# Loading w_down of a decode kernel in three transfers instead of one, two of them issued by GpSimd

## The chip, the cores and the metric

The kernel runs on one core of a Trainium2 chip. The metric is device time in microseconds of one execution, given as the median of several executions. A profile of one execution stands beside the times; its span runs from the first to the last instruction that the profiler records, and is a little shorter than the time.

## The reference

A decode step for two tokens (B = 2, D = 512): the input is normalised, goes in parallel through an attention over a window of a cache and through a gated feed-forward layer, and both are added to the input. All data are float32.

```python
xn = layernorm(x)                                  # x: [2, 1, 512]
# attention: 32 query heads, 8 kv heads, head size 128, the last W = 4096 of 32768 positions
q = (xn @ wq) as [2, 32, 1, 128]                   # wq: [512, 4096]
p = softmax(q @ k_window^T * 128 ** -0.5)
a = (p @ v_window) as [2, 1, 4096] @ wo            # wo: [4096, 512]
# feed-forward, F = 1792
gate = xn @ W_gate                                 # [512, 1792]
gate = gate * (gate > 0)
up = xn @ W_up                                     # [512, 1792]
f = (gate * up) @ W_down                           # W_down: [1792, 512]
out = x + a + f
```

## The kernel before

All large inputs (wq in two halves, w_gate, w_up, 8 tiles of k, 8 tiles of v, w_down and two halves of wo) are loaded by SyncE into one ring of four slots (pool `ring`, RING = 4), each slot of 32 KB in each of the 128 partitions. A load waits on SyncE until the last reader of the tile that had the slot before is done; since SyncE issues in program order, the order of the loads is that of the code: wq0, wq1, w_gate, w_up, then k and v tiles in turn, the last two v tiles, w_down (`wd`), wo0 and wo1. wo1 is cut into five pieces of 8, 4, 2, 1 and 1 blocks (L434). The small input x is loaded by ScalarE (L105). GpSimd makes constants at the start (L113 to L134) and has nothing else to do.

The order of the instructions is that of the code (`manual_schedule`); semaphores are put in by the framework.

The stages, with the names that the profile shows:

- Normalisation and transposition of x (`xt_ps`, L177 to L182), then the query projection (`q_ps`, L190).
- The feed-forward's first part: `g_ps` and `u_ps` (L217) hold gate and up, with a quarter of the 1792 columns in each group of 32 partitions (row 32c + b of the tile is token b, quarter c, FQ = 448 columns). `gr` (L224) is the gate after its comparison, `hh` (L226) the product with up. 56 small matmuls against the identity (L231), for k in 0..13 and quarter c, turn hh into `ht_ps`, where partition p and block k hold hidden unit 14 p + k. The copy at L234 puts it into `hT`, a constant tile of [128, 14, 2, 16] that was set to zero by GpSimd (L120), where only index 0 of the last dimension is filled.
- For each of four groups g = (half of the kv heads, token): 8 x 8 transposes of each k tile (`pk`, L255) with copies by ScalarE and VectorE in turn (`kT`, L244), scores (`s`, L268), softmax (L277 to L321), products with the v tile (`o`, L332), and gathering (`oa`, L348). The scores of one group run beside the softmax and values of the one before.
- The end: `project` (L419) multiplies 17 columns of a block of hT or oT with the matching block of w_down or wo and sums all into one PSUM tile `y_ps`, whose first term is x. First come the values of the last group, then the 14 blocks of w_down (L429), then `spread_heads` (`op`, L362) for the last heads, then 16 blocks of wo0 and 16 of wo1. `yo` (L438) is the copy out of PSUM, and SyncE stores it (L439).

w_down is loaded by `load_down` (L82), one transfer: partition p takes the 14 rows 14 p to 14 p + 13, which lie one behind the other in memory (28 KB).

Of the kernel before, what the change touches and what calls it, by code (L numbers as in the profile page):

```python
# [9 lines left out]
F32 = mybir.dt.float32  # L10
AF = mybir.ActivationFunctionType
ALU = mybir.AluOpType
# [8 lines left out]
def kernel(  # L21
# [12 lines left out]
    nc = tc.nc  # L34
    P = 128
    B, _, D = x.shape
# [3 lines left out]
    F = w_gate.shape[1]  # L40
# [14 lines left out]
    FB = F // P  # L55
    FQ = F // Q
    assert (B, REP, DH, S1, J) == (2, 4, P, 2, 64)

    const = ctx.enter_context(tc.tile_pool(name="const", bufs=1))
    ring = ctx.enter_context(tc.tile_pool(name="ring", bufs=RING))  # L60
    ktp = ctx.enter_context(tc.tile_pool(name="ktp", bufs=2))
    work = ctx.enter_context(tc.tile_pool(name="work", bufs=2))
    ps_kt = ctx.enter_context(tc.tile_pool(name="ps_kt", bufs=3, space=PSUM))
    ps_s = ctx.enter_context(tc.tile_pool(name="ps_s", bufs=1, space=PSUM))
    ps_1 = ctx.enter_context(tc.tile_pool(name="ps_1", bufs=1, space=PSUM))
# [3 lines left out]
    def load(name, src, shape):  # L69
        t = ring.tile(shape, F32, name=name, tag="ring")  # L70
        nc.sync.dma_start(t, src)
        return t
# [6 lines left out]
    def load_ff(w, name):  # L79
        return load(name, w.rearrange("(p k) f -> p k f", p=P), [P, KC, F])  # L80

    def load_down():  # L82
        return load("wd", w_down.rearrange("(p k) e -> p k e", p=P), [P, FB, D])

    def load_kv(cache, name, g, a):
        r, b = divmod(g, B)
# [21 lines left out]
    ident = const.tile([P, P], F32, name="ident")  # L108
# [7 lines left out]
    eps_t = const.tile([32, 1], F32, name="eps_t")  # L116
    nc.vector.memset(eps_t, EPS)

    hT = const.tile([P, FB, B, 16], F32, name="hT")
    nc.gpsimd.memset(hT, 0.0)  # L120
    oT = const.tile([P, R, NJ, B, 16], F32, name="oT")
    nc.gpsimd.memset(oT, 0.0)
# [52 lines left out]
    for kc in range(KC):  # L175
        m, k = divmod(kc, 2)
# [9 lines left out]
    for kc in range(KC):  # L186
        for r in range(R):
            for c in range(C):
                n = r * C + c
                nc.tensor.matmul(  # L190
                    q_ps[r][32 * c:32 * c + 32, :], xnT[:, 0, kc, :], wqt[kc // 2][:, kc % 2, n * 512:(n + 1) * 512],
                    start=(kc == 0), stop=(kc == KC - 1),
# [3 lines left out]
    for r in range(R):  # L196
        qs = work.tile([P, 512], F32, name=f"qs{r}", tag="qs")
# [15 lines left out]
    u_ps = ps_kt.tile([P, FQ], F32, name="u_ps", tag="kt")  # L213
    for dst, wt in ((g_ps, gw), (u_ps, uw)):
        for kc in range(KC):
            for c in range(Q):
                nc.tensor.matmul(  # L217
                    dst[32 * c:32 * c + 32, :], xnT[:, 1, kc, :], wt[:, kc, c * FQ:(c + 1) * FQ],
                    start=(kc == 0), stop=(kc == KC - 1),
# [2 lines left out]
    nc.scalar.copy(gs, g_ps)  # L222
    gr = work.tile([P, FQ], F32, name="gr", tag="gr", bufs=1)
    nc.vector.scalar_tensor_tensor(gr, gs, 0.0, gs, op0=ALU.is_gt, op1=ALU.mult)  # L224
    hh = work.tile([P, FQ], F32, name="hh", tag="qs")
    nc.vector.tensor_tensor(hh, gr, u_ps, op=ALU.mult)  # L226
    ht_ps = ps_1.tile([P, FB, B], F32, name="ht_ps", tag="misc")
    hv = hh.rearrange("p (w k) -> p k w", k=FB)
    for k in range(FB):
        for c in range(Q):  # L230
            nc.tensor.matmul(  # L231
                ht_ps[32 * c:32 * c + 32, k], hv[:, k], ident[:, 32 * c:32 * c + B], start=True, stop=True
            )
    nc.vector.tensor_copy(hT[:, :, :, 0], ht_ps)  # L234

# [115 lines left out]
    def finish(g):  # L353
        r, b = divmod(g, B)
        if b == 0:
            osb[r] = const.tile([HR, B, P], F32, name=f"osb{r}")
        nc.vector.tensor_scalar(osb[r][:, b], oa[g], rls[g], 2.0, op0=ALU.mult, op1=ALU.mult)

    def spread_heads(r):
        op = ps_1.tile([P, NJ, B], F32, name=f"op{r}", tag="misc")  # L360
        for e in range(NE):
            nc.tensor.matmul(  # L362
                op, spread[:, e].rearrange("h k e -> h (k e)"),
                osb[r][:, :, e * NJ:(e + 1) * NJ].rearrange("h b j -> h j b"),
                start=(e == 0), stop=(e == NE - 1),
            )
        nc.vector.tensor_copy(oT[:, r, :, :, 0], op)
# [34 lines left out]
    scores(*pend.pop())  # L402
    vin = [load_kv(v_cache, "v", g, a) for a in range(NP)]
    dw = load_down()
    for _ in softmax(g):
        pass
# [10 lines left out]
    def project(lhsT, w, stop):  # L417
        for e in range(Q):
            nc.tensor.matmul(  # L419
                y_ps[32 * e:32 * e + 17, :], lhsT.rearrange("p b s -> p (b s)")[:, 0:17],  # L420
                w[:, e * P:(e + 1) * P], start=False, stop=stop,
            )
# [2 lines left out]
        values(g, a, vin[a])  # L425
        gather(g, a)
    finish(g)
    for k in range(FB):
        project(hT[:, k], dw[:, k], False)  # L429
    spread_heads(R - 1)  # L430
    for r, cuts in ((0, (0, NJ)), (1, (0, 8, 12, 14, 15, NJ))):
        wt = ring.tile([P, NJ, D], F32, name=f"wo{r}", tag="ring")
# [35 lines left out]
```

## Time and profile before

| what | us |
|---|---|
| median of 3 runs | 232.58 (232.47 to 232.73) |
| profiled execution | 232.63 |
| its span | 230.8 |
| TensorE busy | 180.2 |
| VectorE busy | 66.3 |
| ScalarE busy | 48.3 |
| GpSimd busy | 5.4 |

The page of the profile gives busy times of each engine, a table of the DMA queues (packets, megabytes and the time that packets took, as a share of the 16 load engines over the span), the chain of work that ended last, and groups of instructions by line. q1 is the queue that SyncE fills, q10 ScalarE's, and the queues of kind "instruction" bring the program itself. TensorE appears as PE (matmuls) and PEld (weight loads), VectorE as DVE, ScalarE as ACT, GpSimd as POOL, SyncE as SP; the letter q behind a name is the engine's instruction queue. A float32 matmul of the code appears as two instructions.

### The profile page before, as it was taken

How to read it: one execution, taken by the hardware profiler on the slowest of the kernel's cores; microseconds unless marked ns; L12 is line 12 of the kernel's file. 1: busy time of each engine (PE TensorE's matmuls, PEld its weight loads, DVE VectorE, ACT ScalarE, POOL GpSimd, SP SyncE). 2: the span in 40 equal slices, each digit the busy share in tenths (PEclk: the TensorE clock that was granted, in tenths of full speed). 3: DMA queues.
4: the chain of work that ended last, by engine and by line, in shares of the span. 5: the costliest groups of instructions: out<-in, count | busy, mean ns of one | idle time of the engine just before them, and what ended most of it. 6: DMA issues, size and time to landing. Idle time of an engine off the chain costs nothing.

```text
span 230.8 us, 4036 instructions
## 1 busy us (share of the span) xinstructions
PE 180.2 (78%) x1828; PEld 109.7 (48%) x1828; DVE 66.3 (29%) x131; ACT 48.3 (21%) x81; POOL 5.4 (2%) x21
## 2 busy tenths in 40 slices
PE   0066961749999889998899699889979964888393
PEld 0031230249666573664483566458456522247281
DVE  0320021014444561441472233158034133010000
ACT  2000100004444551440351243044033102100000
POOL 8000000000000000000000000000000000000000
PEclk9999797697999999999999799999999998899678
DMA  7999999999999999999999999999999999999980
GB/s 273 426 403 443 437 432 411 454 435 415 420 452 426 420 423 450 420 429 420 435 432 430 426 432 426 429 437 426 429 426 440 420 437 435 417 435 420 406 341 35
DMA packets 3964, 95.21 MB, mean 413 GB/s; under 512 B 452, under 2 KB 460, under 8 KB 876
## 3 DMA queue, kind: packets, MB, share of 16 engines
q1 hardware_dynamic: 3900, 94.90, 96.4%
q8 instruction: 14, 0.23, 0.4%
q10 hardware_dynamic: 48, 0.07, 0.1%
q14 instruction: 2, 0.02, 0.0%
HBM read 94.96 MB, written 0.00 MB: 412 GB/s over the span
## 4 chain that ended last, share of the span: by engine, by line
DMA 52%; PE 40%; DVE 4%; issue 1%; SPq 1%; ACT 1%
DMA k<-in_A_k_cache_dram 37%; PE pk L255 21%; DMA wo<-in_A_wo_dram 11%; PE s L268 8%; PE o L332 5%; DMA x<-in_A_x_dram 4%; PE q_ps L190 3%; PE pp L312 1%; PE oa L348 1%; SPq L434 1%; DVE kT L244 1%; DVE pt L313 1%; ACT p L301 1%; DVE on L244 0%; DVE m L277 0%
## 5 line engine op out<-in xcount | busy, mean ns | idle before, releaser
L255 PE MATMUL pk<-ident,k 128*128 128x128 f32 x512 | 68.0, 287 | 6.4 <-DMA k<-in_A_k_cache_dram 6.3
L255 PEld LDWEIGHTS pk<-ident,k 128*128 128x128 f32 x512 | 58.2, 146 | 21.2 <-issue 17.1
L244 DVE COPY kT<-pk 128x512 f32<-128x512 f32 x64 | 44.2, 691 | 52.6 <-PE pk L255 46.7
L244 ACT COPY kT<-pk 128x512 f32<-128x512 f32 x64 | 37.5, 586 | 81.5 <-PE pk L255 81.5
L332 PE MATMUL o<-v,pt 128*32 128x512 f32 x256 | 31.0, 615 | 0.0
L268 PE MATMUL s<-kT,qz 128*32 128x512 f32 x256 | 30.9, 598 | 0.0
L332 PEld LDWEIGHTS o<-v,pt 128*32 128x32 f32 x256 | 11.0, 113 | 14.6 <-issue 9.9
L190 PE MATMUL q_ps<-wq,xnT 128*32 128x512 f32 x64 | 11.9, 914 | 2.8 <-DMA wq<-in_A_wq_dram 2.3
L419 PE MATMUL y_ps<-wo,oT 128*17 128x128 f32 x256 | 10.1, 323 | 5.0 <-DMA wo<-in_A_wo_dram 4.8
L268 PEld LDWEIGHTS s<-kT,qz 128*32 128x32 f32 x256 | 7.0, 109 | 11.9 <-issue 11.5
L348 PE MATMUL oa<-on,pick 128*16 128x128 f32 x64 | 8.3, 273 | 4.1 <-DVE on L244 3.3
L419 PEld LDWEIGHTS y_ps<-wo,oT 128*17 128x17 f32 x256 | 7.9, 116 | 7.0 <-DMA wo<-in_A_wo_dram 6.0
L244 DVE COPY on<-o 128x512 f32<-128x512 f32 x4 | 2.8, 692 | 29.0 <-PE o L332 29.0
L348 PEld LDWEIGHTS oa<-on,pick 128*16 128x16 f32 x64 | 5.8, 97 | 11.1 <-DVE on L244 7.0
L177 PE MATMUL xt_ps<-ident,xn 32*128 32x32 f32 x4 | 1.0, 299 | 12.9 <-DVE xn L172 12.9
L217 PE MATMUL u_ps<-wu,xnT 128*32 128x448 f32 x32 | 4.6, 735 | 6.3 <-DMA wu<-in_B_W_up_dram 6.3
L190 PEld LDWEIGHTS q_ps<-wq,xnT 128*32 128x32 f32 x64 | 2.7, 154 | 11.3 <-issue 7.1
L244 ACT COPY on<-o 128x512 f32<-128x512 f32 x4 | 2.3, 586 | 25.5 <-PE o L332 25.5
L301 ACT ACTIVATE p<-s,nm 128x1024 f32<-128x1024 f32 x4 | 4.5, 1115 | 12.5 <-DVE nm L296 12.5
L177 PEld LDWEIGHTS xt_ps<-ident,xn 32*128 32x128 f32 x4 | 0.8, 206 | 12.8 <-issue 12.8
L312 PE MATMUL pp<-ident,p 128*128 128x128 f32 x32 | 4.9, 279 | 2.4 <-ACT p L301 1.5
L313 DVE TENSOR_TENSOR pt<-pp,own 128x512 f32<-128x512 f32 x8 | 5.4, 690 | 3.4 <-PE pp L312 3.4
(71 smaller groups left out, 61.5 us busy)
## 6 DMA issues: line engine op xcount, KB each, us to landing
k<-in_A_k_cache_dram SPq DMA_DIRECT2D x8, 4096.0 KB, 29.2
v<-in_A_v_cache_dram SPq DMA_DIRECT2D x8, 4096.0 KB, 31.2
wq<-in_A_wq_dram SPq DMA_DIRECT2D x2, 4096.0 KB, 17.5
wo<-in_A_wo_dram SPq DMA_DIRECT2D x1, 4096.0 KB, 31.5
wg<-in_B_W_gate_dram SPq DMA_DIRECT2D x1, 3584.0 KB, 30.2
wu<-in_B_W_up_dram SPq DMA_DIRECT2D x1, 3584.0 KB
wd<-in_B_W_down_dram SPq DMA_DIRECT2D x1, 3584.0 KB, 27.9
wo<-in_A_wo_dram SPq DMA_DIRECT2D x1, 2048.0 KB, 21.6
```

Of the source, the lines that this page charges most:

```text
L190: nc.tensor.matmul(q_ps[r][32 * c:32 * c + 32, :], xnT[:, 0, kc, :], wqt[kc // 2][:, kc % 2, n * 512:(n + 1) * 512], start=(kc == 0), stop ...
L217: nc.tensor.matmul(dst[32 * c:32 * c + 32, :], xnT[:, 1, kc, :], wt[:, kc, c * FQ:(c + 1) * FQ], start=(kc == 0), stop=(kc == KC - 1),)
L244: (nc.vector.tensor_copy if turn[0] % 2 else nc.scalar.copy)(dst, src)
L255: nc.tensor.transpose(pk[:, u * P:(u + 1) * P], kt_in[:, j * P:(j + 1) * P], ident)
L268: nc.tensor.matmul(ss[g][32 * q:32 * q + 32, :], qz[:, g, 32 * n:32 * n + 32], kt[:, h, q * 512:(q + 1) * 512], start=(a == 0 and s1 == 0 ...
L301: nc.scalar.activation(p, both, AF.Exp, bias=nm, scale=SCALE, accum_out=l)
L312: nc.tensor.transpose(pp[:, u], pv[:, lo:lo + P], ident)
L313: nc.vector.tensor_tensor(pts[g][:, jh].rearrange("p n u k -> p u n k"), pp.rearrange("p u (n k) -> p u n k", k=HK), own.rearrange("p h i ...
L332: nc.tensor.matmul(o[32 * q:32 * q + 32, :], pts[g][:, jh, n].rearrange("p u k -> p (u k)"), v[:, lo:lo + 512], start=(s1 == 0 and jh == 0 ...
L348: nc.tensor.matmul(oa[g], pick[:, u, 8 - 8 * a:24 - 8 * a], ons[a][:, u], start=(a == 0 and u == 0), stop=(a == NP - 1 and u == 3),)
L419: nc.tensor.matmul(y_ps[32 * e:32 * e + 17, :], lhsT.rearrange("p b s -> p (b s)")[:, 0:17], w[:, e * P:(e + 1) * P], start=False, stop=stop,)
L434: nc.sync.dma_start(wt[:, j0:j1], wo_rows(r, j0, j1))
```

## The change

The 1792 rows of w_down are divided otherwise. They are cut into 16 runs of 112 rows (FR). Of each run the first 104 rows go to eight partitions, 13 rows (FM) in each, by one transfer that SyncE issues as before. The last 8 rows of each run, 128 rows in all, become blocks 13 and 14 of the lower 64 partitions: two transfers of 64 rows (8 runs of 8 rows), one row of 2 KB in a partition, both issued by GpSimd. The tile has 15 blocks for 14, and so has hT.

The hidden units must lie in the same order, so hh is written already ordered: one product for the 13 blocks, another for the last 8 columns of each run; the transposing matmuls of block 13 put quarters 0 and 1 into block 13 and quarters 2 and 3 into block 14, both in the lower 64 partitions; and the copy into hT becomes two. At the end `project` runs over 15 blocks, the last two with 64 rows.

```diff
+    FR = F // 16
+    FM = FB - 1
     def load_down():
-        return load("wd", w_down.rearrange("(p k) e -> p k e", p=P), [P, FB, D])
+        t = ring.tile([P, FB + 1, D], F32, name="wd", tag="ring")
+        runs = w_down.rearrange("(i x) e -> i x e", i=16)
+        main = bass.AP(
+            tensor=w_down.tensor, offset=w_down.offset, ap=[[FR * D, 16], [FM * D, 8], [1, FM * D]]
+        )
+        nc.sync.dma_start(t[:, 0:FM].rearrange("p k e -> p (k e)"), main)
+        for s in range(2):
+            nc.gpsimd.dma_start(t[0:64, FM + s], runs[8 * s:8 * s + 8, 8 * FM:, :])
+        return t
...
-    hT = const.tile([P, FB, B, 16], F32, name="hT")
+    hT = const.tile([P, FB + 1, B, 16], F32, name="hT")
...
-    hh = work.tile([P, FQ], F32, name="hh", tag="qs")
-    nc.vector.tensor_tensor(hh, gr, u_ps, op=ALU.mult)
-    ht_ps = ps_1.tile([P, FB, B], F32, name="ht_ps", tag="misc")
-    hv = hh.rearrange("p (w k) -> p k w", k=FB)
+    hh = work.tile([P, FB, 32], F32, name="hh", tag="qs")
+    gv = gr.rearrange("p (i x) -> p i x", i=4)
+    uv = u_ps.rearrange("p (i x) -> p i x", i=4)
+    nc.vector.tensor_tensor(
+        hh[:, 0:FM].rearrange("p k (i y) -> p i y k", i=4), gv[:, :, 0:8 * FM].rearrange("p i (y k) -> p i y k", y=8),
+        uv[:, :, 0:8 * FM].rearrange("p i (y k) -> p i y k", y=8), op=ALU.mult,
+    )
+    nc.vector.tensor_tensor(
+        hh[:, FM].rearrange("p (i y) -> p i y", i=4), gv[:, :, 8 * FM:], uv[:, :, 8 * FM:], op=ALU.mult
+    )
+    ht_ps = ps_1.tile([P, FB + 1, B], F32, name="ht_ps", tag="misc")
     for k in range(FB):
         for c in range(Q):
+            s = c // 2 if k == FM else 0
             nc.tensor.matmul(
-                ht_ps[32 * c:32 * c + 32, k], hv[:, k], ident[:, 32 * c:32 * c + B], start=True, stop=True
-            )
-    nc.vector.tensor_copy(hT[:, :, :, 0], ht_ps)
+                ht_ps[32 * (c - 2 * s):32 * (c - 2 * s) + 32, k + s], hh[:, k], ident[:, 32 * c:32 * c + B],
+                start=True, stop=True,
+            )
+    nc.vector.tensor_copy(hT[:, 0:FM, :, 0], ht_ps[:, 0:FM])
+    nc.vector.tensor_copy(hT[0:64, FM:, :, 0], ht_ps[0:64, FM:])
...
-    for k in range(FB):
-        project(hT[:, k], dw[:, k], False)
+    for k in range(FB + 1):
+        n = P if k < FM else 64
+        project(hT[0:n, k], dw[0:n, k], False)
```

More of the change, by code (lines that the diff above doesn't have):

```diff
@@ L80, in load_ff @@
         return load(name, w.rearrange("(p k) f -> p k f", p=P), [P, KC, F])
+    FR = F // 16
+    FM = FB - 1
+    assert FR == 8 * FM + 8
     def load_down():
-        return load("wd", w_down.rearrange("(p k) e -> p k e", p=P), [P, FB, D])
+        t = ring.tile([P, FB + 1, D], F32, name="wd", tag="ring")
[7 more added lines that the diff above has]
+        return t
     def load_kv(cache, name, g, a):
```

## The prediction

> **What bounds the kernel now.** I read the queue table of the page first, then the chain of waits at its end, then the stages by window.
>
> ```profile
> span 230.8 us, 4036 instructions
> ...
> PE 180.2 (78%) x1828; PEld 109.7 (48%) x1828; DVE 66.3 (29%) x131; ACT 48.3 (21%) x81; POOL 5.4 (2%) x21
> ...
> ## 3 DMA queue, kind: packets, MB, share of 16 engines
> q1 hardware_dynamic: 3900, 94.90, 96.4%
> q8 instruction: 14, 0.23, 0.4%
> q10 hardware_dynamic: 48, 0.07, 0.1%
> ```
>
> The load engines are busy for 96.4% of the span with SyncE's queue q1 alone. That is 0.964 x 230.8 = 222.5 us in each of 16 engines for 94.90 MB, so 26.7 GB/s for one engine, and 16 KB takes 0.61 us. No compute engine comes near that share. The end of the chain says the same.
>
> ```profile
> 202.21 24.94 DMA wo<-in_A_wo_dram
> 227.15 0.04 issue
> 227.19 0.46 PE y_ps L419 x8
> 227.65 0.02 issue
> 227.68 0.29 DVE yo L438
> ```
>
> The last piece of wo is issued at 202.21 and lands 24.94 us later, because all earlier loads stand ahead of it in the queues. After it come 0.8 us of TensorE and VectorE, and the store of the output. So the time is set by when the last load engine has finished its list, and the windows show how the engines finish (the last two columns are the busy share of the 16 engines and GB/s).
>
> ```profile
> core 0: us, PE busy (x) PEld busy (x) DVE busy (x) ACT busy (x) POOL busy (x), PEclk, DMA share, GB/s
> ...
> 60.00:220.00 160.00, 140.32 (x1313) 87.29 (x1315) 54.70 (x97) 41.54 (x70) 0.00 (x0) 0.96 1.00 429
> ...
> 223.00:224.00 1.00, 1.00 (x46) 0.99 (x40) 0.00 (x0) 0.00 (x0) 0.00 (x0) 1.00 0.73 287
> 224.00:225.00 1.00, 1.00 (x44) 0.96 (x40) 0.00 (x0) 0.00 (x0) 0.00 (x0) 1.00 0.47 184
> 225.00:226.00 1.00, 0.85 (x33) 0.57 (x28) 0.00 (x0) 0.00 (x0) 0.00 (x0) 1.00 0.38 135
> 226.00:227.00 1.00, 0.92 (x24) 0.36 (x18) 0.00 (x0) 0.00 (x0) 0.00 (x0) 1.00 0.17 61
> 227.00:228.00 1.00, 0.41 (x8) 0.13 (x8) 0.29 (x1) 0.00 (x0) 0.00 (x0) 1.00 0.00 0
> ```
>
> From 60 to 220 us the share is 1.00: no engine ever waits for a slot. From 223 us on the share falls to 0.38, which is 0.38 x 16 = 6 engines, and these few hold the end until 227.15. From 223 us an engine still has 0.73 + 0.47 + 0.38 + 0.17 = 1.75 us of work on average, and the latest has 4.15. So the end lies 2.4 us behind an even finish. q1 gives every engine the same bytes; what isn't even is the fetching of instructions, 14 packets of 0.23 MB / 14 = 16 KB, each 0.004 x 230.8 x 16 / 14 = 1.05 us (0.92 to 1.19 by the rounding of 0.4%). Two of them on one engine make 2.1 us, about the lateness seen. I take it that the late engines are those that serve two or more fetches.
>
> **The change, part by part.** *Bytes.* w_down stays 3584 KB: 128 packets of 26 KB on q1 in place of 128 of 28 KB, and 128 packets of 2 KB on GpSimd's queue. If both transfers together give every engine eight 2 KB packets, each engine loses 16 KB on q1 (0.61 us) and gains 16 KB in small packets. The trace has no GpSimd load, so I bound the price of these packets.
>
> The low end is the end of the kernel, where 2 KB packets of wo run alone: 61 GB/s at share 0.17, so 61 / (0.17 x 16) = 22.4 GB/s for one engine. 16 KB then take 0.73 us, **+0.12 us**. For the high end I look at the load of x, 32 packets of 2 KB that come from a second queue while q1 runs, two for each engine.
>
> ```profile
> 6.40:9.70 3.30, 0.00 (x0) 0.00 (x0) 0.74 (x4) 0.00 (x0) 0.00 (x0) 1.00 0.98 390
> ```
>
> ```profile
> x<-in_A_x_dram ACTq DMA_DIRECT2D x1, 64.0 KB, 9.2
> ```
>
> While these packets pass, 390 GB/s flow where 429 do later: (429 - 390) x 3.3 us = 129 KB, 8.0 KB for one engine, 0.30 us lost beside what x itself moves. (This window is short, packets of q1 last over 1 us, so it may be off by half.) If the loss goes with each packet, 0.15 us, eight make 1.2 us: **+1.2 us**. If it goes with one visit of a second queue, it is 0.30 us on top of the 0.12: +0.42 us. The third row is the instruction fetch, also a visit from another queue: 1.05 us for 16 KB against 0.61, +0.44 us. Two rows of three lie near 0.4, so I take **+0.42 us**, on every engine and so on the late ones.
>
> *Which engines.* The trace doesn't say which engine serves a packet. Even shares are my choice; the two uneven cases are rivals below. [...]
>
> *Issue and wait.* GpSimd is done early, and SyncE issues wd as soon as the slot of the last k tile is free.
>
> ```profile
> 5.93 0.17 POOL L134 MEMSET pick<- 128x96 f32 x1
> ```
>
> ```profile
> L71 SPq DMA_DIRECT2D wd<-in_B_W_down_dram x1: 337/337/337, 179.4 to 179.4; - x1
> ...
> DMA to landing us min/median/max: 27.9/27.9/27.9
> ```
>
> The two GpSimd issues wait for the same slot. Nothing is queued behind them on GpSimd but the end of the program, so the wait holds nobody. They go out near 179.4 us. Their queue is its own, so they needn't stand behind the two v tiles that q1 still holds; their packets then pass ahead of v, which lands up to 1.0 us later (0.42 + 0.61), and wd's main part lands about when it did. The sum of bytes in each engine is the same at any order.
>
> [...]
>
> *TensorE at the end.* The rows of the last products (the bracket is idle time before a row):
>
> ```profile
> 195.46 4.88 PE L332 MATMUL o<-v,pt 128*32 128x512 f32 x32
> ...
> 207.38 3.25 PE L419 MATMUL y_ps<-wd,hT 128*17 128x128 f32 x112
> ...
> 210.56 1.97 PE L362 MATMUL op<-osb,spread 16*128 16x32 f32 x16
> ...
> 217.11 9.85 PE L419 MATMUL y_ps<-wo,oT 128*17 128x128 f32 x248 [4.58 <-DMA wo<-in_A_wo_dram]
> ```
>
> The 14 blocks of w_down take 112 matmuls in 3.25 us. Fifteen blocks take 120: 8 more, 3.25 x 8 / 112 = +0.23 us. TensorE then sits idle 4.58 us until wo has landed, which covers this, and also a v or a wd that lands 1.0 us later. If wo came 4.6 us earlier, the 0.23 us would show. So 0 us.
>
> *The hidden layer.* hh becomes two products, hT two copies.
>
> ```profile
> 46.23 0.62 DVE L226 TENSOR_TENSOR hh<-gr,u_ps 128x448 f32<-128x448 f32 x1 [9.70 <-PE u_ps L217]
> ...
> 46.91 1.95 PE L231 MATMUL ht_ps<-ident,hh 128*32 128x2 f32 x112 [0.75 <-DVE hh L226]
> 48.93 0.20 DVE L234 COPY hT<-ht_ps 128x28 f32<-128x28 f32 x1 [2.07 <-PE ht_ps L231]
> ...
> 51.35 8.84 PE L255 MATMUL pk<-ident,k 128*128 128x128 f32 x61 [2.49 <-DMA k<-in_A_k_cache_dram]
> ```
>
> The first product has 416 of 448 columns, 0.58 us by the row; the second, of 32 columns, is near the 28-column copy, 0.20 us; so is the second copy. That is +0.36 us on VectorE, and with a new order of writing up to twice the first product, +0.9. TensorE's 112 small matmuls start up to 0.7 us later and end before the k tile lands (2.49 us idle), so nothing moves. v's load at that time is released by u_ps, not by hh. GpSimd's memset of hT grows by one fifteenth at the start, while everyone waits for x. All 0 us.
>
> *The end of the program* waits for two more transfers, one or two semaphore instructions (x7: 17/28/28 ns in the row below): +0.05 us.
>
> ```profile
> L463 SPq EVENT_SEMAPHORE  x7: 17/28/28, 228.7 to 230.7; - x7
> ```
>
> **Sum.** +0.42 (small packets from a second queue) + 0.05 (end) = +0.47 us. The profiled execution took 232.63 us, 1.8 us of it outside the span; the median of the runs is 232.58. I set the sum on the median: 232.58 + 0.47 = 233.05, which I give as **233.1 us**. 0.2% is 0.47 us, about what a measurement of this kernel can tell from no change, so the forecast lies on that line.
>
> **Rivals.** *A: both transfers run on the same eight engines, and these aren't the ones that fetch instructions.* Then the late engines lose 16 KB, 0.61 us, and gain nothing; the others gain 16 KB and two visits, some 1.5 us, and have over 2 us to spare at the end. 232.58 - 0.61 = **232.0 us**, faster. For it: the 2.4 us of uneven finish. [...] It decides as soon as the engines that finish last get no small packets. Chance 0.12.
>
> *B: both on the same eight, and these are the late ones.* They get 32 KB for 16: +0.61, and twice the price of small packets, +0.84: 232.58 + 1.45 + 0.05 = **234.1 us**. Chance 0.10.
>
> *C: the bare price of the packets.* The loss beside x is that of a first transfer at the start, not of a second queue. +0.12 + 0.05: **232.75 us**, no change that can be told. For it: at 6.4 us q1 is itself young. Against: the fetch packets, late in the kernel, cost as much. Chance 0.28.
>
> *D: the price goes with each packet,* +1.2 us or more: **233.8 us**, up to 236 if a stop of 0.44 us goes with each of eight packets (8 x 0.44 = 3.5). Chance 0.10.
>
> *E: the small transfers land late and TensorE waits.* They may land as late as 217 us without harm, 37 us after their issue: I give it no chance of its own.
>
> **How the numbers follow.** The forecast has 0.40, within about 232.9 to 233.4; more than half of it is beyond the line of 0.2% (233.05). Slower: 0.30 of the forecast's, B and D, 0.50. Same: 0.10 of the forecast's and C, less a little for a gain at the edge, 0.37. Faster: A with that little, 0.13. The range takes in A's 232.0 and B's 234.1 and leaves out the worse part of D and the ends of A and B: 232.0 to 234.2.
>
> **What would show it right or wrong.** A new queue in the queue table with some 128 packets of 2 KB, and q1 smaller by 0.26 MB. If the even case holds, the windows after 223 us keep their shape (0.73, 0.47, 0.38, 0.17), later by under half a microsecond. If A holds, the shares there rise, and the end comes earlier; if B, fewer engines carry a longer tail. The 4.58 us before wo should stay above 3.5, and the transposes of k at 51.35 should stay. The prediction is wrong if instruction fetches fall on other engines than now, or if TensorE's idle time before wo is gone.

## The result, and the profile after

The changed kernel takes 246.26 us (median of 3, 246.25 to 246.41) against 232.58 us: 1.059 times as long, interval 1.0565 to 1.0614. The forecast was 233.1 us with a range of 232.0 to 234.2, so the time lies 12 us above the range. The sign was right, the size wrong by nearly thirty times (13.7 us measured, 0.47 us forecast).

The page of the changed kernel, first its slices (DMA share and GB/s in 40 equal parts of the span) and the queue table:

```profile
span 244.5 us, 4058 instructions
...
DMA  7999999999999999999999999999999998999980
GB/s 263 434 429 459 403 444 412 434 426 429 458 440 434 426 436 426 423 429 426 434 433 429 429 426 429 429 437 423 429 426 365 353 263 180 219 258 426 401 330 26
...
q1 hardware_dynamic: 3900, 94.64, 96.0%
q8 instruction: 14, 0.23, 0.4%
q0 software_dynamic: 160, 0.26, 0.3%
```

The bytes are those of before, 0.26 MB of them now on GpSimd's queue q0. The engines are still called busy for 96.0% of a longer span. But from the 31st slice on the bytes no longer flow at 430 GB/s: 365, 353, 263, 180, 219, 258, and then 426 again. A DMA row of 9 beside 180 to 365 GB/s means that the packets themselves take longer (2.07 us for one of 26 KB, below), and a share of busy time alone would not show it.

The same by stages (last columns: busy share of the load engines, GB/s):

```profile
100.00:180.00 80.00, 73.75 (x626) 46.31 (x629) 31.51 (x54) 23.97 (x42) 0.30 (x1) 0.98 1.00 431
...
184.00:198.00 14.00, 9.26 (x79) 4.26 (x74) 3.94 (x10) 1.20 (x2) 0.00 (x0) 0.82 1.04 359
198.00:222.00 24.00, 11.28 (x84) 3.54 (x80) 1.03 (x2) 0.58 (x1) 0.00 (x0) 0.78 0.98 230
```

The same two late stages of the kernel before:

```profile
184.00:198.00 14.00, 9.09 (x79) 3.71 (x72) 3.85 (x10) 1.21 (x2) 0.00 (x0) 0.88 1.00 428
198.00:222.00 24.00, 17.81 (x296) 12.26 (x292) 1.24 (x3) 0.59 (x1) 0.00 (x0) 0.86 0.99 421
```

Until 180 us the rate is that of before. From 184 to 198 us it lacks 428 - 359 = 69 GB/s, 1.0 MB, which is 2.2 us at 431 GB/s. From 198 to 222 us it lacks 421 - 230 = 191 GB/s, 4.6 MB or 10.6 us. Together 12.9 us of the 13.7. The queue tables give the same for the mean of the 16 load engines (the mean engine, below): its packets took 96.0% + 0.3% of 244.5 us, 235.5 us, where they took 222.5 us before, so 13.0 us more. There are thus two losses, one while GpSimd's rows pass beside the last v tiles, and a larger one while the main part of w_down passes.

What TensorE saw of it (the bracket is idle time before a row and what ended it):

```profile
206.59 5.28 PE L357 MATMUL o<-v,pt 128*32 128x512 f32 x32 [3.31 <-DMA v<-in_A_v_cache_dram]
...
221.56 6.23 PE L444 MATMUL y_ps<-wd,hT 128*17 128x128 f32 x120 [7.82 <-DMA wd<-in_B_W_down_dram]
...
231.04 8.44 PE L444 MATMUL y_ps<-wo,oT 128*17 128x128 f32 x224 [1.35 <-DMA wo<-in_A_wo_dram]
```

w_down comes 14.2 us later than before (221.56 against 207.38), and wo 13.9 us (231.04 against 217.11). TensorE doesn't bound the end: the chain still ends with the landing of wo's last piece, now at 240.89 us (227.15 before). The tail, too, is much like that of before, 13 us later:

```profile
236.00:237.00 1.00, 1.00 (x40) 0.98 (x40) 0.00 (x0) 0.00 (x0) 0.00 (x0) 1.00 0.75 285
237.00:238.00 1.00, 0.95 (x35) 0.76 (x28) 0.00 (x0) 0.00 (x0) 0.00 (x0) 1.00 0.46 182
238.00:239.00 1.00, 0.90 (x35) 0.62 (x31) 0.00 (x0) 0.00 (x0) 0.00 (x0) 1.00 0.41 145
239.00:240.00 1.00, 0.82 (x33) 0.55 (x24) 0.00 (x0) 0.00 (x0) 0.00 (x0) 1.00 0.16 59
240.00:241.00 1.00, 0.76 (x24) 0.20 (x17) 0.00 (x0) 0.00 (x0) 0.00 (x0) 1.00 0.03 10
```

The shares 0.75, 0.46, 0.41, 0.16 stand where 0.73, 0.47, 0.38, 0.17 stood, with a remnant of 0.03 behind them. The mean engine lost 13.0 us and the one that ends last 13.7, so the loss is nearly even, as in the even case of the forecast; it was far more than reckoned.

### The profile page after: what moved, and what is told of

Same layout as the page of the kernel before. It is cut to its first block, busy times and chain, and to the rows that moved or that the text cites. A ratio compares the mean times of both kernels' runs of the same rounds, so it can differ in the third digit from the quotient of the medians.

```text
span 244.5 us, 4058 instructions
## 1 busy us (share of the span) xinstructions
PE 187.2 (77%) x1836; PEld 110.2 (45%) x1836; DVE 66.7 (27%) x133; ACT 48.3 (20%) x81; POOL 6.7 (3%) x23
## 4 chain that ended last, share of the span: by engine, by line
PE 49%; DMA 42%; DVE 4%; ACT 1%; issue 1%; SPq 1%
DMA k<-in_A_k_cache_dram 23%; PE pk L280 23%; DMA wo<-in_A_wo_dram 15%; PE s L293 10%; PE o L357 8%; DMA x<-in_A_x_dram 4%; PE q_ps L205 2%; PE pp L337 2%; PE oa L373 1%; DVE kT L269 1%; ACT p L326 1%; PE op L387 1%; SPq L460 1%; DVE on L269 1%; PE nm_ps L317 0%
## 5 line engine op out<-in xcount | busy, mean ns | idle before, releaser
L357 PE MATMUL o<-v,pt 128*32 128x512 f32 x256 | 33.0, 653 | 3.3 <-DMA v<-in_A_v_cache_dram 3.3
L293 PE MATMUL s<-kT,qz 128*32 128x512 f32 x256 | 31.6, 610 | 0.0
L357 PEld LDWEIGHTS o<-v,pt 128*32 128x32 f32 x256 | 10.6, 119 | 20.7 <-issue 13.5
L205 PE MATMUL q_ps<-wq,xnT 128*32 128x512 f32 x64 | 12.4, 946 | 3.5 <-DMA wq<-in_A_wq_dram 3.0
L293 PEld LDWEIGHTS s<-kT,qz 128*32 128x32 f32 x256 | 7.2, 111 | 12.6 <-issue 12.2
L444 PE MATMUL y_ps<-wd,hT 128*17 128x128 f32 (+1 forms) x120 | 6.2, 398 | 7.8 <-DMA wd<-in_B_W_down_dram 7.8
L232 PE MATMUL u_ps<-wu,xnT 128*32 128x448 f32 x32 | 5.4, 841 | 6.4 <-DMA wu<-in_B_W_up_dram 6.4
L444 PEld LDWEIGHTS y_ps<-wo,oT 128*17 128x17 f32 x256 | 7.4, 109 | 4.1 <-DMA wo<-in_A_wo_dram 3.1
L444 PEld LDWEIGHTS y_ps<-wd,hT 128*17 128x17 f32 (+1 forms) x120 | 4.6, 141 | 9.4 <-DMA wd<-in_B_W_down_dram 8.1
L205 PEld LDWEIGHTS q_ps<-wq,xnT 128*32 128x32 f32 x64 | 2.7, 162 | 12.2 <-issue 7.6
L337 PE MATMUL pp<-ident,p 128*128 128x128 f32 x32 | 5.6, 309 | 2.4 <-ACT p L326 1.5
```

What stands on the lines that cost most here:

```text
L205: nc.tensor.matmul(q_ps[r][32 * c:32 * c + 32, :], xnT[:, 0, kc, :], wqt[kc // 2][:, kc % 2, n * 512:(n + 1) * 512], start=(kc == 0), stop ...
L232: nc.tensor.matmul(dst[32 * c:32 * c + 32, :], xnT[:, 1, kc, :], wt[:, kc, c * FQ:(c + 1) * FQ], start=(kc == 0), stop=(kc == KC - 1),)
L293: nc.tensor.matmul(ss[g][32 * q:32 * q + 32, :], qz[:, g, 32 * n:32 * n + 32], kt[:, h, q * 512:(q + 1) * 512], start=(a == 0 and s1 == 0 ...
L337: nc.tensor.transpose(pp[:, u], pv[:, lo:lo + P], ident)
L357: nc.tensor.matmul(o[32 * q:32 * q + 32, :], pts[g][:, jh, n].rearrange("p u k -> p (u k)"), v[:, lo:lo + 512], start=(s1 == 0 and jh == 0 ...
L444: nc.tensor.matmul(y_ps[32 * e:32 * e + 17, :], lhsT.rearrange("p b s -> p (b s)")[:, 0:17], w[:, e * P:(e + 1) * P], start=False, stop=stop,)
```

## The experiments

In the packet records of the trace a 26 KB packet of the changed kernel's main part takes 2.07 us on average, where 1.00 us would be its share at 26.7 GB/s. Three causes offer themselves: GpSimd's queue, the addresses read, and the division of the transfer among engines and partitions. All times below are medians beside runs of the kernel before on the same chip (232.38 to 232.49 us).

**Main part and small transfers, each undone.** Small transfers by SyncE, the main part as changed:

```diff
-            nc.gpsimd.dma_start(t[0:64, FM + s], runs[8 * s:8 * s + 8, 8 * FM:, :])
+            nc.sync.dma_start(t[0:64, FM + s], runs[8 * s:8 * s + 8, 8 * FM:, :])
```

> The changed kernel, but SyncE issues the two small transfers; the main part keeps its 16 x 8 source. Theory T (two separate costs: about 10 us because the source of the main part has 16 as its outermost dimension, so that each load engine writes eight adjacent partitions and the engines meet at the same entries of SBUF; about 3 us because GpSimd's packets lengthen the packets of q1 beside them): 243.5 us, the packets of 26 KB still near 2.0 us and the v packets before them at 1.2 us. Rival R1 (GpSimd's queue upsets the load engines and both slow stretches are its doing): 232.8 us. Rival R2 (the addresses in memory, a step of 26 KB, make the main part slow): 243.5 us, as T.

Measured: 242.72 us (1.045, 1.042 to 1.0481), 26 KB packets at 2.01 us, 261 GB/s from 198 to 222 us. The large loss is there without GpSimd; R1 falls. Next, GpSimd as in the change, and the main part with 128 outermost:

```diff
-            tensor=w_down.tensor, offset=w_down.offset, ap=[[FR * D, 16], [FM * D, 8], [1, FM * D]]
+            tensor=w_down.tensor, offset=w_down.offset, ap=[[FB * D, P], [1, FM * D]]
```

> The changed kernel with GpSimd's two transfers as they are, but the main part reads 26 KB of each 28 KB with 128 as the outermost dimension of its source (13 of 14 rows of each partition's old run, so the rows meet other hidden units than in the reference: the sum is not that of the reference). T: 235.6 us, a slow stretch of v packets while GpSimd's packets pass, none after. R1: 246 us. R2: 235.6 us if the step in memory matters, 246 us if the packet size of 26 KB does.

Measured: 234.07 us (1.0078, 1.0049 to 1.0107), packets at 1.00 us. Its stages:

```profile
184.00:198.00 14.00, 9.27 (x76) 4.17 (x72) 3.93 (x10) 1.21 (x2) 0.00 (x0) 0.82 1.00 366
198.00:222.00 24.00, 17.70 (x272) 11.30 (x268) 1.24 (x3) 0.59 (x1) 0.00 (x0) 0.86 0.99 422
```

The second loss is gone (422 GB/s where 230 stood), the first remains (366). The time is 1.5 us below the 235.6 of T and of R2's first case. A packet of 26 KB is not slow in itself. Then both edits:

> Both edits at once: main part with 128 outermost (as in the run before the last, the rows meet other hidden units), small transfers by SyncE. [...] R1: 232.8 us. R2: 232.8 us by the step, 243.5 us by the packet size.

Measured: 232.86 us (1.0032, 0.9998 to 1.0067; single runs from 232.67 to 234.69). Both of T's costs are taken away here, and the time lies within 0.5 us of the kernel before. A slow stretch is there even so: the profiled execution, which took 233.38 us, moved 307 GB/s from 202 to 208 us, where the kernel before moved 436. The small rows by SyncE pass there; more of this below. The price of the main part's shape is 9.9 us with SyncE's small rows (242.72 against 232.86) and 12.2 us with GpSimd's (246.26 against 234.07). So the two costs don't simply add; what makes the 2.3 us more was not followed. And the kernel before with only the shape of its one source written as 16 x 8:

```diff
-        return load("wd", w_down.rearrange("(p k) e -> p k e", p=P), [P, FB, D])
+            tensor=w_down.tensor, offset=w_down.offset, ap=[[8 * FB * D, 16], [FB * D, 8], [1, FB * D]]
```

> The kernel before, one transfer of 28 KB to each partition from the same addresses, with only the shape of its source changed from 128 runs to 16 x 8 runs. T: 28 KB packets at some 2.1 us, 243 us. R1 and R2: 232.6 us, since neither GpSimd nor an address is changed. If the two dimensions are merged into one on the way to the chip, 232.6 us under T too, with packets at 1.07 us, and the run tells nothing.

Measured: 232.37 us (1.0, 0.9989 to 1.0011). This run tells nothing: its issue took as long as a plain one (336 ns against 337), so I take it that the two dimensions, which follow each other without a gap, had been merged into 128. In the change they can't be (8 x 13 rows are not 112), and there SyncE's issue takes 581 ns. The rows of the issue, in this run and in the changed kernel:

```profile
L87 SPq DMA_DIRECT2D wd<-in_B_W_down_dram x1: 336/336/336, 179.5 to 179.5; - x1
```

```profile
L95 SPq DMA_DIRECT2D wd<-in_B_W_down_dram x1: 581/581/581, 179.4 to 179.4; - x1
```

**Which side is slow, memory or SBUF?** Four kernels with the small transfers on SyncE and only the source of the main part (or its destination) changed. First 32 runs of four partitions, then 16 x 8 with half the step, then 128 with twice the step, then two halves:

```diff
+ap=[[56 * D, 32], [FM * D, 4], [1, FM * D]]
```

> Main part with a source of 32 runs x 4 pieces of 26 KB (runs 56 rows apart; the rows meet other hidden units, so the sum is not that of the reference), small transfers by SyncE. Theory S (the slow main part is a matter of the SBUF side: 16 as outermost dimension gives each load engine eight adjacent partitions, and then several engines write at the same time where only one can): if groups of four partitions keep the engines apart, 26 KB packets at 1.0 us and 232.9 us; if an engine still takes eight adjacent ones, 2.0 us and 242.7 us. Rival M (a matter of memory: with 16 x 8 the engines read at the same time at addresses 224 KB apart): 232.9 us, since the runs are 112 KB apart. Rival U (any source of unmerged dimensions is slow): 242.7 us.

```diff
+ap=[[4 * FB * D, 16], [FB * D, 8], [1, FM * D]]
```

> Main part with a source of 16 x 8 pieces of 26 KB, but the 16 runs only 112 KB apart, so that neighbouring runs overlap (half of w_down is read twice, half not at all; the sum is not that of the reference), small transfers by SyncE. S: 242.7 us, 26 KB packets at 2.0 us. M: 232.9 us, packets at 1.0 us. U: 242.7 us.

```diff
+tensor=wo.tensor, offset=wo.offset, ap=[[28 * D, P], [1, FM * D]]
```

> Main part with 128 as outermost dimension, pieces of 26 KB that are 56 KB apart, read out of wo in place of w_down (which is too small for that step; the sum is not that of the reference), small transfers by SyncE. [...] S: 232.9 us, packets at 1.0 us. [...] U: 232.9 us.

```diff
+        for y in range(2):
+            main = bass.AP(
+                tensor=w_down.tensor, offset=w_down.offset + y * 64 * FB * D, ap=[[FB * D, 64], [1, FM * D]]
+            )
+            nc.sync.dma_start(t[64 * y:64 * y + 64, 0:FM].rearrange("p k e -> p (k e)"), main)
```

> Main part as two transfers of 64 partitions each (0 to 63, then 64 to 127), each with a plain source of 64 pieces of 26 KB (13 of 14 rows, the rows meet other hidden units, so the sum is not that of the reference), small transfers by SyncE. S: all engines write to one half of the partitions at a time, so the packets take up to 2.0 us and the kernel some 242 us; less where the engines are out of step. M and U: 232.9 us, packets at 1.0 us.

Measured: 233.1 us for 32 x 4 (1.0028, 1.0004 to 1.0052), 242.73 us for 16 x 8 at half the step (1.0437, 1.0407 to 1.0467), 233.0 us for 128 at the wide step (1.0027, 1.0016 to 1.0039), 243.1 us for the two halves (1.0453, 1.0423 to 1.0483). The stage from 198 to 222 us of each, in this order:

```profile
198.00:222.00 24.00, 18.50 (x300) 12.09 (x296) 1.24 (x3) 0.59 (x1) 0.00 (x0) 0.80 0.99 389
```

```profile
198.00:222.00 24.00, 12.74 (x152) 6.94 (x148) 1.03 (x2) 0.58 (x1) 0.00 (x0) 0.78 0.99 259
```

```profile
198.00:222.00 24.00, 18.95 (x304) 12.18 (x300) 1.24 (x3) 0.58 (x1) 0.00 (x0) 0.80 1.00 395
```

```profile
198.00:222.00 24.00, 11.87 (x144) 6.96 (x140) 1.03 (x2) 0.59 (x1) 0.00 (x0) 0.78 0.99 263
```

Two at some 390, two at some 260 GB/s (421 before), with the load engines busy throughout in all four (shares of 0.99 and 1.00), so it isn't that fewer of them worked. 16 x 8 stays slow with its runs 112 KB apart in place of 224, where M had 232.9 us, and 128 stays fast with its pieces 56 KB apart in place of 28: the time follows the shape, not the addresses, and M falls. R2 falls with it: pieces with a step of 26 KB are fast as 32 x 4, and pieces with a step of 28 KB slow as 16 x 8. U falls by 32 x 4, which wasn't merged either (its issue takes 535 ns, a plain one 337) and is fast; so are all k and v loads (64 x 2, 1.22 us for a packet of 32 KB). And a plain transfer to 64 partitions is as slow as 16 x 8 (packets at 1.96 us), without any odd shape. S is the one theory left that fits all four times.

What the runs show of it is the cost of two shapes: a transfer to 64 partitions and a source of 16 x 8 run at half rate, with 2.0 us for a packet of 26 KB in both where 128 outermost takes 1.00. That the cause lies in which partitions are written at one moment, and how T and S divide them among the engines, is the author's inference from these shapes and times: the trace names no engine and no partition.

**The smaller loss.** Is it GpSimd's? Two more transfers by GpSimd, into the upper 64 partitions:

```diff
+        for s in range(2):
+            nc.gpsimd.dma_start(t[64:P, FM + s], runs[8 * s:8 * s + 8, 8 * FM:, :])
```

> As the run with 128 outermost and GpSimd's two transfers (234.07 us), with two more such transfers by GpSimd into unused rows of the upper 64 partitions (256 KB more; main part's rows still meet other hidden units). Theory G1 (each packet of GpSimd's queue costs its engine time): the stretch of slow v packets, 14 us long there, becomes twice as long, and the price of 1.7 us doubles, plus 0.6 us for the bytes: 236.4 us. Rival G2 (a fixed price for using that queue at all): 234.7 us. Rival G3 (the small packets are slow because all of them go to the lower 64 partitions): the two added transfers cost little beside their bytes, 234.8 us.

Measured: 236.92 us (1.0202, 1.018 to 1.0224), near G1's 236.4, with the slow stretch about doubled (357 GB/s from 184 to 198 us and 375 from 198 to 212, where the run with two transfers has 366 and 434). G2 and G3 fall. The added rows went to 64 partitions as well, only to the upper ones; this matters below. Then half of GpSimd's work, and none, with ScalarE in its place:

```diff
+            (nc.sync if s else nc.gpsimd).dma_start(t[0:64, FM + s], runs[8 * s:8 * s + 8, 8 * FM:, :])
```

> As the run with 128 outermost and GpSimd's two transfers, but the second of them is issued by SyncE. G1: half of the price, 233.2 us, the slow stretch of v packets ends near 190 us instead of 198. G2: 234.0 us. G3: 234.0 us, nothing changes but the place.

```diff
+            nc.scalar.dma_start(t[0:64, FM + s], runs[8 * s:8 * s + 8, 8 * FM:, :])
```

> As the run with 128 outermost, but both small transfers are issued by ScalarE, whose queue is a second hardware queue like that of x. G1 with a price that goes with any second queue: 234.1 us. G1 with a price of GpSimd's software queue alone: 232.9 us, v packets at 1.2 us beside them. G3: 234.1 us.

Measured: 234.29 us (single runs 233.24 to 234.83) and 233.99 us (232.49 to 234.47). Both scatter by more than what they were to tell apart, so their times decide nothing. The trace of the first does show something: the slow stretch ends near 191 us, as G1 said (378 GB/s until then, 431 from 191 to 198), and a shallower one (392 GB/s) comes from 204 to 212 us, where SyncE's half passes. The trace of the second is of its shortest execution (232.49 us) and shows little. Then the change with 32 runs of four partitions and the reference's sum:

```diff
+    FR = F // 32
+ap=[[FR * D, 32], [FM * D, 4], [1, FM * D]]
+            nc.gpsimd.dma_start(t[0:64, FM + s], runs[16 * s:16 * s + 16, 4 * FM:, :])
```

> The change with its reference sum, but w_down cut into 32 runs of 56 rows: 52 rows of each go to four partitions, 13 rows in each, and the last 4 rows of the 32 runs are the 128 small rows, still by two transfers of GpSimd. By the theory of the SBUF side the main part runs at full rate, by G1 GpSimd's price remains: 234.0 us. If GpSimd's packets were the cause of the slow main part after all, 245 us.

Measured: 233.46 us (1.0043, 1.0027 to 1.0059). So four partitions in a run instead of eight (and small rows in runs of 4 instead of 8) take back 12.8 of the 13.7 us. And the same without GpSimd:

> The kernel of the run before (32 runs of 56 rows, with its reference sum), but SyncE issues the two small transfers; nothing of GpSimd is left. G1 (each packet of GpSimd's queue costs about 0.17 us on its engine; that kernel has six for each engine, and lost 1.0 us): 232.6 us, the v packets at full rate from 184 to 198 us. If what is left of the loss comes from the fifteenth block, the split hidden layer or the 2 KB packets themselves: 233.4 us, as with GpSimd.

Measured: 233.73 us (1.0056, 1.0043 to 1.007), no better than with GpSimd. The loss only moves, from where GpSimd's rows pass to where SyncE's do. First the kernel with GpSimd, then the one without:

```profile
184.00:191.00 7.00, 4.74 (x41) 1.94 (x33) 2.17 (x5) 0.00 (x0) 0.00 (x0) 1.00 1.00 362
...
204.00:212.00 8.00, 7.17 (x148) 4.78 (x144) 1.03 (x2) 0.00 (x0) 0.00 (x0) 1.00 1.03 443
```

```profile
184.00:191.00 7.00, 4.56 (x46) 1.89 (x37) 2.22 (x6) 0.00 (x0) 0.00 (x0) 1.00 1.00 431
...
204.00:212.00 8.00, 7.17 (x154) 4.84 (x146) 1.03 (x2) 0.00 (x0) 0.00 (x0) 1.00 1.00 363
```

That is (431 - 362) x 7 = 0.48 MB in one and (443 - 363) x 8 = 0.64 MB in the other, to be taken roughly, since a packet of 32 KB counts whole in such short windows. G1 falls as it stood: whoever issues these rows, they cost. The last two runs send a fourteenth row to all 128 partitions:

```diff
+        rows = w_down.rearrange("(p k) e -> p k e", p=P)
+        nc.sync.dma_start(t[:, 0:FB - 1], rows[:, 0:FB - 1])
+        nc.gpsimd.dma_start(t[:, FB - 1], rows[:, FB - 1])
```

> The kernel before, with w_down still 14 rows in each of 128 partitions, but 13 of them by SyncE and the fourteenth, 2 KB in every partition, by one transfer of GpSimd: as many small bytes from GpSimd as in the change, to all 128 partitions instead of 64. Theory P (GpSimd's packets cost their engine about 0.17 us each, five or more for each engine): 233.4 us, v packets slowed for some 6 us from 184 us on. Theory H (small rows are dear because a transfer to 64 partitions reaches half of SBUF at a time, whoever issues it): 232.6 us, with at most a trace of slow v packets.

> The same with the fourteenth row issued by SyncE. P and H: 232.5 us, 0.1 us over the kernel before for the 2 KB packets (84 ns for 2 KB where a share of a 28 KB packet is 76 ns, eight of them). If 2 KB rows beside 32 KB packets are dear in themselves, wherever they go: 233.5 us.

Measured: 232.61 us by GpSimd (1.0009, 1.0 to 1.0018), 232.38 us by SyncE (0.9999, 0.999 to 1.0008). The run by GpSimd, queue and stage:

```profile
q0 software_dynamic: 80, 0.26, 0.3%
```

```profile
184.00:191.00 7.00, 4.59 (x46) 1.88 (x37) 2.19 (x6) 0.00 (x0) 0.00 (x0) 1.00 1.03 437
```

The same 0.26 MB from GpSimd pass at 437 GB/s. The queue tables put all these runs side by side. The share of q1 and q0 times the span is the time that the mean engine spent in packets (good to some 0.2 us):

| small rows | partitions | share x span, us | in packets, us | median, us |
|---|---|---|---|---|
| none (kernel before) | | 96.4% x 230.8 | 222.5 | 232.4 to 232.5 |
| 8 x 8 by GpSimd, main part 128 | 64 | 96.6% x 232.2 | 224.3 | 234.07 |
| 8 x 8 by SyncE, main part 128 | 64 | 96.9% x 231.6 | 224.4 | 232.86 |
| 16 x 4 by GpSimd, main part 32 x 4 | 64 | 96.4% x 231.7 | 223.4 | 233.46 |
| 16 x 4 by SyncE, main part 32 x 4 | 64 | 96.6% x 231.8 | 223.9 | 233.73 |
| fourteenth row by GpSimd | 128 | 96.4% x 230.5 | 222.2 | 232.61 |
| fourteenth row by SyncE | 128 | 96.4% x 230.6 | 222.3 | 232.38 |

Rows to 64 partitions cost the mean engine 0.9 to 1.9 us, rows to 128 nothing that can be seen, and within each pair it changes at most 0.5 us who issues them. H's price holds against P's: neither 2 KB rows nor GpSimd are dear, a transfer to 64 partitions is; why it is, no run shows. The last two runs differ from the others also in the number of transfers and of blocks; that the loss sits in the very stage where the rows pass speaks for the partitions. The time doesn't follow the mean engine in one row: 8 x 8 by SyncE costs it as much as by GpSimd, and yet the median rises by 0.5 us and not by 1.7. The time is set by the engine that ends last, and the trace doesn't tell which engines these rows fell on, so this stays open.

If the 0.26 MB alone went at half rate, the time of 0.26 MB would be lost. What was lost was that of 0.48 to 0.64 MB, and of 0.9 MB ((431 - 366) x 14) where the source was 8 x 8; so the packets of other tiles beside these rows are slowed as well. The packet records show it: while GpSimd's 8 x 8 rows passed, v's packets of 32 KB took 1.4 to 1.5 us on average, 1.22 before. How much of that goes with the 64 partitions, and how much with the shape, stays open.

No version tried beats the kernel before; the one with the fourteenth row by SyncE equals it.

## Why the prediction was wrong

- *What bounds the kernel* was right: the load engines, with the tail of late ones. It was right, too, that a dearer transfer would pass undiminished into the time: 13.0 us more in the packets of the mean engine gave 13.7 us.
- **The step that failed is "Bytes":** "128 packets of 26 KB on q1 in place of 128 of 28 KB", each of which was charged at 26.7 GB/s. The new form of the source was in the diff, and I treated it as nothing but another size of packet. It ran at half the rate, 2.07 us for a packet in place of 1.00: +9.9 us in the pair that differs in it alone with SyncE's small rows (242.72 against 232.86), +12.2 us in the pair with GpSimd's (246.26 against 234.07). No rival had it, so that the sign came out right is luck.
- *The price of small packets from a second queue*, +0.42 us read off the load of x, was charged to the wrong cause, and the row doesn't carry it. The same stretch begun 0.1 us earlier shows 421 GB/s in place of 390, and a stretch of the same length after the load of x shows 377. Packets seem to count whole there (a share above 1 can come out no other way), so windows this short scatter by more than the 39 GB/s that were read from them:

```profile
6.30:9.60 3.30, 0.00 (x0) 0.00 (x0) 0.84 (x4) 0.00 (x0) 0.00 (x0) 1.00 1.05 421
```

```profile
13.00:16.30 3.30, 2.79 (x20) 1.34 (x24) 0.42 (x1) 0.00 (x0) 0.00 (x0) 1.00 0.88 377
```

GpSimd's queue costs 0.15 us where its rows go to 128 partitions (232.61 against 232.46; the interval of 1.0 to 1.0018 reaches to 0.42 us, so it doesn't decide between 0.12 and 0.42). What the small rows of the change did cost, 0.5 to 1.7 us of time and 0.9 to 1.9 us of the mean engine, goes with their 64 partitions, and SyncE's transfers pay it as well. In size this is near rival D, but the price doesn't go with each packet: 80 packets to 128 partitions cost the 0.15 us.

- *Which engines:* the even case, as far as the shares of the tail show it: the last engine lost 0.7 us more than the mean. Nothing speaks for A or B, whose 0.6 to 1.5 us would be hard to see beside 13 us. No run shows the eight engines that their terms rest on; nor does one show that q1 gives every engine the same bytes, or that the late engines are those with two or more fetches, which were the author's estimates. The trace names no engine; it shows the shares of the tail above.
- *Issue and wait:* right for the small transfers, wrong for v. The two issues went out at 179.7 and 180.4 us, and the rows landed 10.9 and 17.7 us later, long before their use. But v came more than 1.0 us late: TensorE waited 3.31 us for it, until 206.59. The last v packets passed beside those of the main part, where they took up to 3.6 us, 1.22 before.
- *TensorE at the end:* the cover of 4.58 us, which "should stay above 3.5", shrank to 1.35 us, and still hid everything, also that 120 matmuls took 6.23 us and not 3.48.
- *The hidden layer:* right. The products took 0.86 and 0.18 us (0.62 before), inside the forecast's bounds, and TensorE still waits for k, until 51.51 us.

## What to carry to other kernels

When a transfer's source gets another shape, its bytes and packets don't tell its speed: packets of 26 KB took 2.07 us here with one shape and 1.00 us with another. Pieces of 26 KB to 64 partitions (1.96 us a packet), or in a source of 16 x 8 (2.01 and 2.07 us), ran at half rate. 128 outermost (1.00 us), 64 x 2 (1.22 us for 32 KB) and 32 x 4 (436 GB/s from 198 to 212 us beside 435 before, in the run with GpSimd's rows) ran at full rate. So time the new shape by itself, to the partitions that it is to fill. This kernel, which lives on its transfers, paid for it almost to the last microsecond; look for a low GB/s row under a full DMA row, as 180 under 9 here.

## What else the runs showed

- TensorE's matmuls of one form lasted 273 ns before and 421 ns for w_down in the changed kernel, right after 7.8 us of waiting; the granted clock there was low (0.62):

```profile
224.00:228.00 4.00, 4.00 (x83) 2.93 (x75) 0.00 (x0) 0.00 (x0) 0.00 (x0) 0.62 0.93 393
```

- The 112 small matmuls that follow hh became faster when it was written already ordered, 1.14 us against 1.95: a weight load took 109 ns where it took 162, at a granted clock of 1.00 in both. In the code the weights now lie side by side, with a step of 14 before; that this is the cause was not tested alone.

```profile
48.06 1.14 PE L254 MATMUL ht_ps<-ident,hh 128*32 128x2 f32 x112 [0.99 <-DVE hh L247]
```

- GpSimd's transfers of 8 runs leave 160 packets in its queue, of which 64 carry rows (4 KB each, where the forecast had 128 of 2 KB), 64 carry 8 bytes and 32 four; those of 16 runs leave 96, without the ones of 8 bytes.
